# RWKV7 attention and a SoLU expert layer on one core: the head's first product in 64x64 tiles, an order of three tile shapes, and inverse steps in halves

## The chip, the cores and the metric

The kernel runs on one core of a Trainium2 chip. Five engines of that core work side by side, each on its own list of instructions: TensorE (PE, matrix products, with a separate row PEld for the loading of its weights), VectorE (DVE), ScalarE (ACT), GpSimd (POOL) and SyncE (SP), which here only issues DMAs. The metric is the time of one execution in microseconds (us), as the device measures it; lower is better.

## The reference

Two blocks follow one another. The first is a linear recurrence over 768 time steps, for 4 batches and 8 heads of 40 channels, all in fp32:

```
for t in range(S):
    y[:, :, t] = einsum('bhd,bhde->bhe', rt, state)
    Sa = einsum('bhde,bhe->bhd', state, at)
    state = state * wt[:, :, None, :] - einsum('bhd,bhe->bhde', Sa, bt) + einsum('bhd,bhe->bhde', vt, kt)
```

Its result, rearranged to 3072 tokens of 320 numbers (8 heads of 40), is `x` of the second block:

```
h = x @ w_in                                   # 3072 x 1024
e = exp(h - max(h)); solu = h * e / (sum(e) + 1e-9)
ln = (solu - mean(solu)) / sqrt(var(solu) + 1e-6) * g_ln
out = ln @ w_out                               # 3072 x 320
```

`w_in` (320x1024), `w_out` and `g_ln` arrive as float64 and are narrowed on the chip.

## The kernel before, in words

**Runs.** The sequence is cut into chunks of 64 tokens. A run is one chunk of two batches, so there are 24 runs (12 chunks, 2 pairs of batches) of 128 tokens each, and each is 16 units (2 batches x 8 heads) of 64 tokens by 40 channels. Within a run the recurrence is solved in closed form: the products of a and b of a unit's tokens make a triangular 64x64 matrix, whose inverse gives all of the run's updates at once; only the state goes from a run to the next one of its pair.

**Products of units.** A unit's matrices are at most 64x64, so `mm` (L276) issues them in 64x64 quarters of the 128x128 array, in an order that goes round the four quarters. Names of the groups on TensorE, which the profile uses: pu (solve), ps (scores), psr and px (the state's part), py (norm, which gives the triangular matrix nt, and couple), pz (close), pyo (read, in two parts: with lv and with lu). Transposes (L363) turn a, b, r, k, v, the decay ei and the state: pa, pb, pr, pkv, pst. pcum (L344) sums the logarithms of the decay.

**The inverse.** nt's two 32x32 diagonal blocks per unit are inverted on VectorE, for two runs at a time (GRP = 2): 64 blocks, in 12 inverses. The norm of a run is evicted as nt (L436) and written to DRAM by four DMAs (L444, on POOL but for runs 2 and 3, on SP). Once both runs are there, `blk` is read back with one block to a partition (L453). Then come 30 steps, a generator from which the schedule draws so many at a time. Step j multiplies one column of the block by the columns found (L469, into `prod`) and subtracts (L471):

```
m, n_c = Q - 1 - j, (j + 1) // 2
nc.vector.tensor_tensor(out=t, in0=nb[..j..], in1=u[:, 0:n_c, j:j + 1]..., op=ALU.mult)
nc.vector.tensor_tensor(out=u[:, 0:n_c, j + 1:Q], in0=u[...], in1=t, op=ALU.subtract)
```

A step works on n_c x m elements a partition, from 30 to 126. The result goes to DRAM by SP (L477), and `bring` (L490, L492) fetches each run's part of it back as tu and uh, also by SP, which waits for the write. `flip` (L498) transposes 32x32 blocks of tu.

**The head.** `leave` sums what a run read (tot, L656, VectorE), multiplies it by the decay into x (L664, two on POOL) and into the next state (L674, two on POOL), and moves x into xT, the tokens' channels on partitions (L669, L670: four DMAs on SP; `left`, L684 and L686: six on POOL, a slot later). `hidden` is h = x w_in, 128 tokens by 1024: two products with all 128 rows and one with 64 rows, for each 512 columns. Each fp32 product is two records on TensorE, so h has 12 records a run. Then follow nmax (L706, VectorE), exp (L714, ScalarE), the weighing of h by e (L722, VectorE), the Square that gives the spread (L735, ScalarE, written over h), var and rs (L736, L737), eight transposes of both halves (plnT, L747) with one eviction lnT (L750), the product po with w2 (L761, eight products, in two calls of four), its scaling by rs into osb (L765, ScalarE) and the output's DMAs (L768, SP).

**Order.** The order on every engine is written out by hand. A loop over slots i = -1 to 27 issues in slot i: solve and read of run i, the scores, couple, close and driven of run i+1, the front (a, b, decay, norm) of run i+5, h of run i-3 and the output of run i-4, besides loads of later runs. `bring(i+1)` and the loads of v and r (L299) stand at a slot's start, then w, b, a, k. A table `plans` says how many inverse steps VectorE does at each of six places of a slot (in steady slots 3 + 11, and 2 more in even ones, plus what is left of an inverse), and in the first slots where w_in and w_out are narrowed. The norm of an odd run begins the next inverse.

**PSUM.** There are four pairs of banks, A, B, C and h. A group that takes a pair waits until its last user is read. h and Square have pair h; pu, pa, py, pyo, pz and plnT share A; ps, po, pkv and pcum share B; px, psr, pst and pr share C.

Of the kernel before, what the change touches and what calls it, by code (L numbers as in the profile page):

```python
# [20 lines left out]
IN_ROWS = (((0, 80), (240, 280), (160, 168)), ((80, 160), (280, 320), (200, 208)), ((168, 200), (208, 240)))  # L21
# [3 lines left out]
LAG = 1  # L25
# [5 lines left out]
def shape_constants():  # L31
# [8 lines left out]
        neg_hi=-(row >= Q).astype(np.float64),  # L40
# [10 lines left out]
def kernel(  # L51
# [26 lines left out]
    NK = 3  # L78
# [5 lines left out]
    small = ctx.enter_context(tc.tile_pool(name="small", bufs=3))  # L84
# [33 lines left out]
    a_t = zeroed(nc.vector, "a", [P, H, C], 4, pad)  # L118
# [15 lines left out]
    nc.gpsimd.memset(above, 0.0)  # L134
    for x in range(Q // 2):
        nc.gpsimd.memset(above[:, x, 2 * x + 1:], -1.0)
    w_in = const.tile([P, 2 * NK - 1, DFF // 2], FP32, name="w_in")
# [15 lines left out]
    lands = [(0, 0), (1, 0), (2, 0), (0, 1), (1, 1)]  # L153
    landed = {}

    def land(n, queue):
# [3 lines left out]
        if n < len(lands):  # L160
            kt, x = lands[n]
# [5 lines left out]
            y = 0  # L167
            for at in (x,) if kt < 2 else (0, 1):
                for first, last in IN_ROWS[kt]:
                    queue.dma_start(out=to[y:y + last - first], in_=moe_w_in[first:last, 512 * at:512 * at + 512])  # L170
                    y += last - first
            landed[n] = [(w_in[:, 2 * kt + x], to, None)]
# [50 lines left out]
    def vector(plan, kept=0):  # L223

        for word in plan.split():
            if word in "bsf":
                dict(b=begin_narrow, s=scale_narrow, f=end_narrow)[word]()
            else:
                some(int(word), kept)

    def turn_g():
        pg = pair("B", "pg")[:, 0]
# [9 lines left out]
    def mean_of(lo, hi, begun, tag):  # L242
        t = pair(tag, "pmean")[:, 0]
        nc.tensor.matmul(t[:, 0:DM], lhsT=ident, rhs=begun, start=True, stop=False)
        mean_part(t, lo, hi, False)
        return mean_kept(t)
# [59 lines left out]
    def load_keys(i, names, queue=nc.sync):  # L306
        if not ok(i):
            return
        for n, ap in (("w", w), ("b", b), ("a", a), ("k", k)):
            if n in names:  # L310
                x = a_t[i % 4] if n == "a" else two.tile([P, H, D], FP32, tag="raw_" + n, name="raw_" + n,
                                                             bufs=3)
# [3 lines left out]
    def load_values(i):  # L316
# [4 lines left out]
        d["raw_r"] = two.tile([P, H, D], FP32, tag="raw_r", name="raw_r")  # L321
        load(d["lv"][:, :, C:], v, i)
        load(d["raw_r"], r, i, nc.gpsimd)
# [13 lines left out]
    def decay(i):  # L337
        if not ok(i):
            return
# [3 lines left out]
        t = (pair("B", "pcum")[:, 0] if i > 9 else h_pair("pcum"))[:, 0:DM]  # L343
        nc.tensor.matmul(t, lhsT=c_("cum"), rhs=d["lw"], start=True, stop=True)  # L344
        nc.scalar.activation(out=ei_t[0][:, :, 0:D], in_=heads(t), func=AF.Exp)
        inv = d["inv"] = two.tile([P, DM], FP32, tag="inv", name="inv", bufs=4)
        nc.scalar.activation(out=inv, in_=t, func=AF.Exp, scale=-1.0)  # L347
# [44 lines left out]
    def front_b(i, t=None, y=0):  # L392
# [5 lines left out]
        def evict():  # L398
            d["bT"] = kept("bT", t)
# [18 lines left out]
    def shared_pair(i):  # L418

        if i not in shared:  # L420
            shared[i] = pair("A", "py")
        return shared[i]

    def norm(i, first=lambda: None):
        if not ok(i):
            first()
# [8 lines left out]
        first()  # L435
        nc.scalar.copy(out=nt, in_=t[:, :, 4 * Q:4 * Q + 256].rearrange("p b (j c) -> p b j c", j=4))  # L436
# [3 lines left out]
        queue = nc.sync if 1 < i < 4 else nc.gpsimd  # L440
        for x in range(2):
            for e in range(2):
                home = C * x + Q * e
                queue.dma_start(out=blocks[n][e].rearrange("(a x h) s c -> a x s h c", a=GRP, x=2)[at, x],  # L444
# [11 lines left out]
    def invert(n):  # L456
# [8 lines left out]
        for j in range(1, Q - 1):  # L465
            m, n_c = Q - 1 - j, (j + 1) // 2
            prod = two.tile([P, Q * Q // 8], FP32, tag="prod", name="prod", bufs=1)
            t = prod[:, 0:n_c * m].rearrange("p (c r) -> p c r", c=n_c)
            nc.vector.tensor_tensor(out=t, in0=nb[:, j:j + 1, j + 1:Q].to_broadcast([P, n_c, m]),  # L469
# [498 lines left out]
```

## Time and profile before

| | |
|---|---|
| median of 3 executions | 579.21 us (579.07 to 583.95) |
| profiled execution, span | 580.2 us |
| busy in that span | PE 510.6, PEld 360.5, DVE 407.9, ACT 316.9, POOL 299.8 us |
| slot 0 begins (its pu) | 63.7 us |
| slots 0 to 4 | 115.7 us |
| slots 5 to 18 | 274.3 us, 19.6 each |
| slots 19 to 22 | 75.5 us |
| from 529.2 to the end | 51.0 us |

One execution was recorded by the hardware profiler, and all durations are from it; its span is a microsecond more than the median. A line such as "317.78 0.88 PE pu L276 x32" of the chain (what released what, followed back from the last instruction) says: from 317.78 us on, for 0.88 us, the end waited for PE's 32 records of the group pu, issued in line 276. In the rows of the timeline the tile's name is output<-inputs, followed by the shapes (partitions x elements), and the brackets name the idle time ahead and what ended it. PEclk is TensorE's granted clock as a share of its full speed. SPq, POOLq and the like are the issuing of DMAs on that engine's list.

### The profile page before, as it was taken

Reading aid. Unit: us, or ns where it says so; the run is one execution under the profiler, and the core shown is the slowest. Engines: PE = TensorE matmul, PEld = TensorE weight load, DVE = VectorE, ACT = ScalarE, POOL = GpSimd, SP = SyncE. Lnnn points to the kernel's source line nnn. Section 1 sums busy time; section 2 is a strip of 40 time slices with the busy share of each in tenths; the row PEclk is TensorE's granted clock in tenths of the full one; section 3 lists DMA queues with packets and bytes.
Section 4 is the critical chain, followed back from the end, with each engine's and each line's share of the span. In section 5 each row is a group of like instructions: output and inputs, shape, how many; then the busy total and the mean of one; then the engine's idle time right before and its main releaser. Section 6 shows DMA issues by size and latency. Waiting matters only on the chain.

```text
span 580.2 us, 25261 instructions
## 1 busy us (share of the span) xinstructions
PE 510.6 (88%) x10773; PEld 360.5 (62%) x10773; DVE 407.9 (70%) x1072; ACT 316.9 (55%) x618; POOL 299.8 (52%) x534
## 2 busy tenths in 40 slices
PE   4462764876989999999999999999999989999995
PEld 3241653654766777677667767777777657666543
DVE  4698986996894886877959869779688487332121
ACT  4633573755646565756566566656564455444533
POOL 4554484555635736648576467475773554233200
PEclk9656787879779999999999999999999989999999
DMA  7896886746605536637555475365431431311110
GB/s 152 151 155 135 175 183 114 148 94 113 112 16 124 111 74 134 118 63 141 103 104 114 90 143 113 65 137 105 99 77 39 106 74 32 62 33 27 27 24 23
DMA packets 188200, 56.71 MB, mean 98 GB/s; under 512 B 171680, under 2 KB 181512, under 8 KB 188088
## 3 DMA queue, kind: packets, MB, share of 16 engines
q1 hardware_dynamic: 173288, 36.98, 34.6%
q0 software_dynamic: 12368, 17.19, 12.9%
q8 instruction: 85, 1.39, 1.0%
q10 hardware_dynamic: 2432, 0.92, 0.8%
q14 instruction: 27, 0.22, 0.1%
HBM read 40.10 MB, written 10.22 MB: 87 GB/s over the span
## 4 chain that ended last, share of the span: by engine, by line
PE 65%; DVE 17%; DMA 9%; issue 3%; ACT 3%; SPq 2%; POOL 1%; ACTq 0%; DVEq 0%; POOLq 0%
PE h L276 19%; PE po L761 15%; PE px L276 5%; DVE uu L471 5%; DVE prod L469 5%; PE pyo L276 4%; DMA uu_dram<-uu 3%; PE py L276 3%; PE ps L276 3%; PE pu L276 3%; PE pz L276 2%; PE pkv L363 2%; DMA tu<-uu_dram 2%; PE plnT L747 2%; PE psr L276 2%
## 5 line engine op out<-in xcount | busy, mean ns | idle before, releaser
L276 PE MATMUL h<-w_in,xT 128*128 128x512 f32 (+1 forms) x288 | 123.6, 632 | 0.3
L761 PE MATMUL po<-w,lnT 128*128 128x320 f32 x384 | 118.2, 454 | 1.8 <-ACT lnT L750 1.8
L471 DVE TENSOR_TENSOR uu<-uu,prod 128x30 f32<-128x30 f32 (+4 forms) x360 | 106.2, 295 | 12.4
L469 DVE TENSOR_TENSOR prod<-blk,uu 128x30 f32<-128x30 f32 (+4 forms) x360 | 105.5, 293 | 11.4 <-POOL kb L356 0.7
L664 POOL TENSOR_TENSOR x<-tot,ex 104x256 f32<-104x256 f32 x48 | 32.3, 690 | 130.3 <-DVE tot L656 119.5
L761 PEld LDWEIGHTS po<-w,lnT 128*128 128x128 f32 x384 | 71.3, 194 | 31.9 <-issue 3.2
L444 POOL DMA_DIRECT2D nt_dram<-nt x88 | 52.3, 602 | 24.3 <-ACT c L734 21.4
L276 PEld LDWEIGHTS h<-w_in,xT 128*128 128x128 f32 (+1 forms) x288 | 40.4, 190 | 34.3 <-issue 29.1
L706 DVE TENSOR_REDUCE nmax<-h 128x1 f32<-128x1024 f32 x24 | 29.4, 1224 | 38.0 <-PE h L276 37.5
L510 ACT ACTIVATE wy<-py,cst 128x256 f32<-128x256 f32 x24 | 11.4, 474 | 79.0 <-PE py L276 79.0
L403 DVE TENSOR_TENSOR lu<-pu,cst 128x512 f32<-128x512 f32 x24 | 16.5, 688 | 51.6 <-PE pu L276 51.6
L686 POOL DMA_DIRECT2D xT<-x x96 | 48.7, 511 | 1.2 <-DMA blk<-nt_dram 1.2
L276 PE MATMUL py<-tu,nt 64*64 64x32 f32 x768 | 16.5, 226 | 28.0 <-DVE tot L656 11.6
L714 ACT ACTIVATE e<-h,nmax 128x1024 f32<-128x1024 f32 x24 | 26.8, 1117 | 20.4 <-DVE nmax L706 20.3
L299 POOL DMA_DIRECT2D raw_r<-in_r_dram x48 | 33.8, 707 | 1.4 <-issue 1.3
L276 PEld LDWEIGHTS py<-tu,nt 64*64 64x64 f32 x768 | 15.6, 145 | 30.3 <-issue 19.8
L344 PE MATMUL pcum<-lw,cst 128*128 128x320 f32 x48 | 21.7, 538 | 14.4 <-ACT lw L335 14.4
L737 POOL TENSOR_TENSOR rs<-var,mhalf 128x1 f32<-128x1 f32 x24 | 13.6, 567 | 39.5 <-ACT var L736 38.8
L356 POOL TENSOR_TENSOR kb<-raw_b,inv 128x320 f32<-128x320 f32 x24 | 21.1, 880 | 21.1 <-ACT inv L347 6.9
L722 DVE SCALAR_TENSOR_TENSOR e<-h,e 128x1024 f32<-128x1024 f32 x24 | 29.2, 1215 | 3.8 <-ACT e L714 3.8
L276 PEld LDWEIGHTS pu<-x,tu 64*64 64x64 f32 x768 | 19.5, 142 | 16.8 <-ACT kvT L536 13.7
L735 ACT ACTIVATE h<-e,mu 128x1024 f32<-128x1024 f32 x24 | 26.8, 1116 | 4.1 <-DVE e L722 4.1
(131 smaller groups left out, 1068.9 us busy)
## 6 DMA issues: line engine op xcount, KB each, us to landing
blk<-nt_dram POOLq DMA_DIRECT2D x22, 256.0 KB, 3.7
raw_w<-in_w_dram SPq DMA_DIRECT2D x48, 80.0 KB
a<-in_a_dram SPq DMA_DIRECT2D x48, 80.0 KB
raw_r<-in_r_dram POOLq DMA_DIRECT2D x48, 80.0 KB, 3.5
lv<-in_v_dram SPq DMA_DIRECT2D x48, 80.0 KB
out_dram<-osb SPq DMA_DIRECT2D x47, 80.0 KB
raw_b<-in_b_dram SPq DMA_DIRECT2D x44, 80.0 KB
raw_k<-in_k_dram SPq DMA_DIRECT2D x42, 80.0 KB
```

The lines of the kernel that those rows point to most:

```text
L276: nc.tensor.matmul(o, lhsT=lhsT, rhs=rhs, start=start, stop=stop, skip_group_check=True)
L299: queue.dma_start(out=x[half(p), :, 0:D], in_=ap[2 * bp + p, :, ci * C:(ci + 1) * C, :].rearrange("h t d -> t h d"))
L444: queue.dma_start(out=blocks[n][e].rearrange("(a x h) s c -> a x s h c", a=GRP, x=2)[at, x], in_=nt[home:home + Q].rearrange("p h j c -> p ...
L469: nc.vector.tensor_tensor(out=t, in0=nb[:, j:j + 1, j + 1:Q].to_broadcast([P, n_c, m]), in1=u[:, 0:n_c, j:j + 1].to_broadcast([P, n_c, m]) ...
L471: nc.vector.tensor_tensor(out=u[:, 0:n_c, j + 1:Q], in0=u[:, 0:n_c, j + 1:Q], in1=t, op=ALU.subtract)
L664: nc.gpsimd.tensor_tensor(out=x[0:W2, 2 * q:2 * q + 2].rearrange("p g (b t) -> p b g t", b=2), in0=by_q(tot, q)[:, :, :, 0:C], in1=ex[:, : ...
L686: nc.gpsimd.dma_start(out=xT[to:to + Q, 2], in_=x[at + P - 3 * D:at + D, 2])
L706: nc.vector.tensor_reduce(out=nmax, in_=d["h"], axis=AX.X, op=ALU.max, negate=True)
L714: nc.scalar.activation(out=e, in_=d["h"], func=AF.Exp, bias=d["nmax"], accum_out=d["esum"])
L722: nc.vector.scalar_tensor_tensor(out=d["e"], in0=d["h"], scalar=1.0 / DFF, in1=d["e"], op0=ALU.mult, op1=ALU.mult, accum_out=d["mu"])
L735: nc.scalar.activation(out=d["h"], in_=d["e"], func=AF.Square, scale=-float(DFF), bias=d["mu"], accum_out=sq)
L761: nc.tensor.matmul(t, lhsT=d["lnT"][:, f, :], rhs=w2[:, f, :], start=f == 0, stop=f == NF - 1)
```

## The change

1. **h in 64x64 tiles.** `w_in` is laid out as five groups of 64 rows, both halves of its columns on the two partition halves. `hidden(i, n)` issues for n = 0 to 4 four products of 64 rows by 64 tokens with 512 columns, one in each quarter of the array: 20 products of a run instead of 6. xT holds each group of channels twice, on both partition halves; `moved` writes it with six DMAs on SP, and `left` with six on POOL. The five parts of h are dealt out between the groups of units.
2. **The slot's order.** First all transposes (64 rows by 104 or 128 columns), then everything in 64x64 (h0, pu, ps, h1, psr, norm, h2, carried px, pyo with lv, h3, couple, h4, close, driven px, pyo with lu), then the two groups on the full array (pcum, po undivided).
3. **Inverse steps.** nt is negated when it is evicted, so steps add. Steps with fewer than three columns take one fused instruction for each column; the others are cut into two halves of the columns, two products and two sums.
4. **Engines.** x and the next state (four instructions) go from POOL to VectorE, osb and (from run 10 on) bT from ScalarE to VectorE. Of the four nt writes two go by SP and two by POOL (from run 4 on).
5. **PSUM.** plnT and Square take pair h, each in its turn; pu, py and pcum go to C, px and po to B, psr to A; pz shares py's pair.
6. **Places.** `bring(i+2)` stands at the end of slot i, after all that is left of its inverse's steps; the loads of v and r of run i+3, one run further ahead. The plans are dealt anew: 14 steps in odd and 16 in even steady slots. What stood before the loop for the scores of run 0 is done in slot -1, and w_in and w_out are narrowed at other places. Fewer buffers: raw_w 2 instead of 3, a 3 instead of 4, small ones 2 instead of 3. LAG counts anew (`c = i - LAG`): h is still that of run i-3.

The core of the diff:

```diff
     def norm(i):
-        nc.scalar.copy(out=nt, in_=t[...])
+        nc.scalar.mul(out=nt, in_=t[...], mul=-1.0)
-        queue = nc.sync if 1 < i < 4 else nc.gpsimd
         for x in range(2):
             for e in range(2):
+                queue = (nc.sync, nc.gpsimd)[e] if i > 3 else nc.sync if 1 < i else nc.gpsimd
...
     def invert(n):
         for j in range(1, Q - 1):
             m, n_c = Q - 1 - j, (j + 1) // 2
-            nc.vector.tensor_tensor(out=t, in0=nb[...], in1=u[:, 0:n_c, j:j + 1]..., op=ALU.mult)
-            nc.vector.tensor_tensor(out=u[:, 0:n_c, j + 1:Q], in0=u[...], in1=t, op=ALU.subtract)
+            if n_c < 3:
+                for c in range(n_c):
+                    nc.vector.scalar_tensor_tensor(out=u[:, c, j + 1:Q], in0=nb[:, j, j + 1:Q], scalar=u[:, c, j:j + 1],
+                                                   in1=u[:, c, j + 1:Q], op0=ALU.mult, op1=ALU.add)
+            else:
+                parts_ = ((0, n_c // 2), (n_c // 2, n_c))
+                for lo, hi in parts_:
+                    prod = two.tile([P, 72], FP32, tag="prod", name="prod")
+                    ...
+                    nc.vector.tensor_tensor(out=ts[-1], in0=nb[...], in1=u[:, lo:hi, j:j + 1]..., op=ALU.mult)
+                for x, (lo, hi) in zip(ts, parts_):
+                    nc.vector.tensor_tensor(out=u[:, lo:hi, j + 1:Q], in0=u[:, lo:hi, j + 1:Q], in1=x, op=ALU.add)
...
+    def leave(i, tot):
+        for q in range(2 * (ci < NCH - 1)):
+            nc.vector.tensor_tensor(out=by_q(state_of(i)[:, 1], q)..., op=ALU.mult)
         for q in range(2):
-            nc.gpsimd.tensor_tensor(out=x[...], ..., op=ALU.mult)
+            nc.vector.tensor_tensor(out=x[...], ..., op=ALU.mult)
+        moved(i, 0, nc.sync)
+
+    def moved(i, y, queue):
+        x, xT = st[i]["x"], st[i]["xT"]
+        at = C * y
+        queue.dma_start(out=xT[at:at + D, 0:4], in_=x[0:D])
+        queue.dma_start(out=xT[at + D:at + C, 0:4], in_=x[C:C + C - D])
+        for j in range(4):
+            queue.dma_start(out=xT[at + 16 * j:at + 16 * j + 16, 4], in_=x[C + C - D:C + D, j])
...
+    def hidden(i, n):
+        if n == 0:
+            d["h"] = pair("h", "h").rearrange("p a b -> p (a b)")
+        for y in range(2):
+            for x in (y, 1 - y):
+                mm(d["h"][half(y), 512 * x:512 * x + 512], d["xT"][half(x), n, half(y)], w_in[half(x), n],
+                   start=n == 0, stop=n == NK - 1)
...
-        nc.scalar.activation(out=d["h"], in_=d["e"], func=AF.Square, ...)
+        nc.scalar.activation(out=pair("h", "sq")..., in_=d["e"], func=AF.Square, ...)
-        t = pair("A", "plnT")
+        t = pair("h", "plnT")
-        nc.scalar.activation(out=osb, in_=t, func=AF.Copy, scale=d["rs"])
+        nc.vector.tensor_scalar(out=osb, in0=t, scalar1=d["rs"], scalar2=None, op0=ALU.mult)
```

The main loop after, without its first slots' special cases:

```
load_keys(j + 3, "w"); load_r(i + 3)
front, attend_r, folded, decay_turned, front_b, attend_kv    # transposes, and their evictions
vector(plan[0]); stated(i + 1); left(i - 1)
hidden(c, 0); solved(i); vector(plan[1])
load_keys(j + 2, "bak")
scores(i + 1); flip(i + 1)
hidden(c, 1); scaled(j + 1); stated_r(i + 1); norm(j)         # odd j: begins the next inverse
hidden(c, 2); carried(i + 1); read(i, 0)
load_values(i + 3); logged(j + 2); vector(plan[2])
hidden(c, 3); couple(i + 1); hidden(c, 4); highest(c)
close(i + 1); driven(i + 1); read(i, 1)
exped(c); vector(plan[3]); summed(i); vector(plan[4])
decay(j + 2); weighed(c); spreadof(c); by_value(i + 2)
some(Q, (i + 2) // GRP); bring(i + 2)                         # the rest of that inverse, then its way back
leave(i); vector(plan[5]); output(c - 1)
```

with the steady plans

```diff
-plan = plans.get(i, ("", "", "3", "", "11", "") if i % GRP else ("", "2", "3", "", "11", ""))
+plan = plans.get(i, ("4", "", "7", "1", "", "2") if i % GRP else ("4", "", "o10", "", "", "1"))
```

## Prediction

> **What bounds the kernel now.** I read the page's busy shares and chain shares first, then busy time by stage.
>
> ```profile
> PE 510.6 (88%) x10773; PEld 360.5 (62%) x10773; DVE 407.9 (70%) x1072; ACT 316.9 (55%) x618; POOL 299.8 (52%) x534
> PE 65%; DVE 17%; DMA 9%; issue 3%; ACT 3%; SPq 2%; POOL 1%; ACTq 0%; DVEq 0%; POOLq 0%
> ```
>
> TensorE leads, but VectorE and the DMA hold a quarter of the chain. The windows below are cut at the starts of slots 0, 5 and 19 (their pu) and at 529.2, where the last heads are left; columns: window, its length, busy us of PE, PEld, DVE, ACT and POOL (instructions), PEclk, DMA share, GB/s.
>
> ```profile
> 63.70:179.40 115.70, 87.47 (x2077) 66.66 (x2075) 94.29 (x247) 64.65 (x131) 67.29 (x111) 0.83 0.59 120
> 179.40:453.70 274.30, 273.70 (x6349) 195.63 (x6348) 216.35 (x574) 167.27 (x330) 165.41 (x290) 1.00 0.52 102
> 453.70:529.20 75.50, 72.72 (x1565) 50.16 (x1564) 39.06 (x98) 37.34 (x69) 30.01 (x55) 0.98 0.27 60
> 529.20:580.20 51.00, 44.84 (x285) 25.44 (x284) 11.52 (x15) 18.59 (x34) 6.59 (x12) 1.00 0.09 21
> ```
>
> In slots 5 to 18 PE is never idle (273.7 of 274.3): 14 slots of 19.6 us, with 15.5 of VectorE. There only PE's time counts. Slots 0 to 4 are bound elsewhere (VectorE 94 of 116, half clocks), and the end is a serial chain. The chain of one steady slot (317.8 to 337.4) is PE alone; part of it:
>
> ```profile
> 318.65 0.93 PE ps L276 x64
> 319.59 1.06 PE h L276 x4
> 320.64 0.45 PE pst L363 x16
> 321.09 0.45 PE pa L363 x16
> 321.54 1.91 PE h L276 x4
> ```
>
> **PE, part by part.** I compared each group's time with the spacing of its own records inside it. A full h pair streams in 4 x 0.427 = 1.71 and takes 1.91; the half-row pair 0.85 and takes 1.06; eight po records 2.15 and take 2.35; pu 0.72 and takes 0.88; psr 0.45 and takes 0.63. Where the tile's shape is the same as before it (ps after pu, pa after pst) nothing is lost. So about 0.17 us goes at each change of shape. The chain of a slot has ten changes: 19.6 = 17.7 streaming + 1.9. The new order has three (64x128, 64x64, full): 17.7 + 3 x 0.17 = 18.2, and with 0.1 for what is not counted **T = 18.3**, a gain of 1.3 per slot if PE stays the bound.
>
> h itself should cost the same: 20 matmuls of 64x64, two records each, four abreast, are 10 rounds of 0.427 = 4.3; before 8 full records + 2 rounds of half-row pairs = 10 x 0.427. That four run abreast is seen in pu (32 records of 104 columns in 0.72, four per 0.0895 us = 0.86 ns a column, the rate of po's 0.2685 for 320). No row has 64x64 groups at 512 columns: bounds 4.3 and, two abreast, 8.6. I take 4.3, by pu, the row of the same shape.
>
> **VectorE.**
>
> ```profile
> 300.04 0.69 DVE L403 TENSOR_TENSOR psi<-ps,cst 128x512 f32<-128x512 f32 x1 [0.24 <-PE ps L276]
> 300.65 0.68 DVE L403 TENSOR_TENSOR lv<-ps,cst 128x512 f32<-128x512 f32 x1
> ...
> 306.68 0.19 DVE L469 TENSOR_TENSOR prod<-blk,uu 128x30 f32<-128x30 f32 x1
> 306.90 0.19 DVE L471 TENSOR_TENSOR uu<-uu,prod 128x30 f32<-128x30 f32 x1
> ...
> 313.25 0.27 DVE L469 TENSOR_TENSOR prod<-blk,uu 128x110 f32<-128x110 f32 x1
> 313.56 0.27 DVE L471 TENSOR_TENSOR uu<-uu,prod 128x110 f32<-128x110 f32 x1
> ```
>
> 30 elements take 0.19, 110 take 0.27: 0.16 + 0.001 per element. A dependent one follows 0.035 after the end; psi and lv, independent, overlap by 0.08. A step has a mean of 87 elements, so before: 2 x (0.16 + 0.09 + 0.035) = 0.57, 17.0 an inverse. After, four instructions of 0.205: starts at 0, 0.12, 0.24, 0.36, and the next step at 0.48, since each half waits only for its own half. 26 x 0.48, four short ones of 0.23 to 0.35 and the start: 14.1. That saves 2.9 per inverse, 1.45 a slot. Moved to VectorE: x 2 x 0.34 (256 elements by the same formula, less the overlap), st 2 x 0.24, osb 0.45, bT 0.6 (as aT's 0.69, one input less): +2.2. Gone with them is the stretching of steps that ran against x and st on POOL (a 126-element step at 316.3 took 1.11 and 0.84 instead of 0.28): 11.6 us in 12 inverses, 0.5 a slot. VectorE goes from 15.5 to some 16, 16.6 with flip's waits: under T, hidden beside PE. ACT loses osb and bT and gains nothing.
>
> A rule speaks against the halves. The Trainium skill, "VectorE: DVE Perf Modes", section "The DRAIN you can't avoid", says that the next operation does not start until the pipeline is empty, and asks for fewer operations instead of fewer semaphores. By it a step of four instructions is 0.82 instead of 0.48. The trace disagrees in part: lv starts 0.08 before psi's end.
>
> **SP's queue** decides, I think, how much of PE's gain is kept.
>
> ```profile
> 295.95 1.91 SPq L477 DMA_DIRECT2D uu_dram<-uu  x2
> ...
> 302.73 0.99 SPq L490 DMA_DIRECT2D tu<-uu_dram  x2
> 303.76 0.91 SPq L492 DMA_DIRECT2D uh<-uu_dram  x2
> ```
>
> The inverse goes out in 1.9 (1.3 elsewhere), lands 4.9 later, and comes back as tu and uh; SP waits in between. In the new order this bring stands behind the forced end of the inverse and ahead of everything of the next slot: xT (now 6 on SP instead of 4, before the outputs), the loads of w, b, a, k, v, and two of the four nt writes (4 were POOL's). SP per two slots: ten load pairs 1.35 = 13.5, outputs 2.4, tu and uh 3.8, uu 1.6, nt 4 x 0.45 = 1.8, xT 12 x 0.65 = 7.8, the wait 4.9: 35.8 of 36.6. From the inverse's end in an even slot (16.2) through that list to the second run's nt write is 34.5; with 2.1 of landing and 4.2 for blk's issue and landing (0.54, 3.7), blk is there at 57.0. The next inverse's first operation stands on VectorE at 17.3 of the next even slot, ahead of osb, aT and bT: 36.6 + 17.3 = 53.9. So it is 3.1 late per pair. The stall shifts slot and queue alike and gives the next round more room: bounds 0 and 3.1 a pair; I take the middle, 1.55. **T = 19.1**, 0.5 gained per slot, with bounds 18.3 and 19.85 (where 2T holds the whole round).
>
> POOL loses x, st and two nt writes and gains two xT: its 11.8 busy a slot falls, and what it hides (kb, blk) stays hidden. raw_w and a with one buffer fewer cost nothing while SP is behind, since it loads later anyway; if not, they are in the 3.1.
>
> **The other stages.** Before slot 0: attend_kv(0), attend_r(0) and scores(0) move into slot -1, beside VectorE's and the first inverse's waits: -2, bounds 0 and -4. Slots 0 to 4: 80 inverse steps at 0.1 to 0.15 less are -8 to -12, the moved operations 5 x 1.3 = +6.5, fewer half clocks: -4, bounds -12 and +4, for VectorE is 82% busy there. Slots 19 to 22 have no more loads, and took 22.5, 17.9, 17.9 and 17.1 (the first with 2.8 idle and 3.4 at half clock): after, 4 x 16.8 = 67.3 instead of 75.5, -8, since no inverse is late there; bound -3. The tail's period, from one h to the next, is h 4.97, nmax 1.24, exp 1.22, weighing 1.25, Square 1.25 = 10.06. Now the transposes and their eviction use h's PSUM pair ahead of the next h: +0.65 + 1.05, while h, all 64x64, needs 0.6 less: 11.1, times nearly four: +4, bounds +1 and +6.
>
> **Sum**, on the profiled 580.2: -2 - 4 - 14 x 0.5 - 8 + 4 = 563. The median of three is 1.0 below the profiled span: **562**.
>
> **Rivals.**
> *PE holds throughout* (0.20): blk is early because SP's issues are shorter than their means; T = 18.4: 14 x 0.7 more gives 552, and slots 0 to 4 with 2 more 550. For it: DMA share 0.52, so the queue is not bandwidth. Against: the 35.8 of 36.6.
> *The round takes it all* (0.13): T = 19.85, and slots 0 to 4 bound by the same round, no gain: -2 + 3.5 - 8 + 4 = 577.5, so 577.
> *Slower: the clock* (0.18). SP's load pairs have steady means of 1.32 to 1.61; with them the list is 37.1 instead of 35.8, and late blk stops VectorE, then PE through aT and bT. From an idle time of some 1.8 us on, the clock halves:
>
> ```profile
> 168.16 1.08 PE L276 MATMUL py<-tu,nt 64*64 64x32 f32 x32 [1.84 <-DVE tot L656]
> 170.07 4.63 PE L761 MATMUL po<-w,lnT 128*128 128x320 f32 x8
> ```
>
> Here 1.84 idle is followed by 6.8 us at half clock (po 4.63 instead of 2.35), 3.3 lost. Once a pair, at the even slot's end, with the stall of 1.55: T = 18.3 + (1.55 + 3.3) / 2 = 20.7, 14 x 1.1 = +15, slots 0 to 4 at -2: -2 - 2 + 15 - 8 + 4 = +7, **587**. It decides between 1.55 and 1.84, which is close; an idle time of 0.5 at 269.6 cost no clock.
> The Trainium skill, "TensorE: Matmul & The Clock Gate", section "Why this matters for your kernels", allows idle gaps up to about 3 us; by it this case would lose only the stall and end near 563. The trace disagrees: 1.84 was enough.
> *Halves that don't overlap* (0.04): each instruction waits out the one before as the dependent pair at 306.7 does, and a step is 4 x 0.24 = 0.96 instead of 0.57, +0.39 x 26 / 2 = 5 a slot on VectorE, 21.6 with its waits: T = 22, 14 x 2.4 = +34, and +12 in the head: about 625.
> *h not four abreast* (0.03): +4.3 a slot where PE is the bound, T near 22.6: some 630.
>
> **Chances.** The forecast 0.42 (552 to 572), the rivals as given. A per cent, 5.8 us, is about what a measurement here tells from no change. Faster by over 1%: the forecast and PE holding, 0.62; within 1% (574 to 585): the round's 0.13 and the clock's lower end, 0.02, together 0.15; slower: the rest of the clock's 0.16, and the last two, 0.23. The range, 546 to 588, takes in the first four cases and leaves out 2 in 10: the last two, the clock's upper half, and PE with the head's bound of -12.
>
> **What would show it.** Right: pu to pu 19.1 in the steady slots; ten rounds of h at 4.3 to 4.4; three jumps of 0.17 a slot; steps at 0.47; at the ends of even slots an idle PE of 1 to 2 us behind VectorE's wait for blk, and SP without a pause but that for uu. T of 18.4 and no wait on blk would mean the queue was overrated; half clocks in the steady slots, the slower rival; a tail under 54, that the shared pair costs nothing. Wrong altogether if VectorE is busy over 18 us a slot, or the first five slots take over 120.

## The result, and the profile after

The changed kernel takes **606.56 us** (median; 600.84 to 608.89 in 4 executions), the kernel before 580.35 beside it. The ratio is **1.0436, 95% interval 1.0373 to 1.0500**: 4.4% slower, where 562 was forecast. The profiled execution has a span of 607.1 us against 580.2. Cut at the same points as before (the first record of pu in slots 0, 5, 19 and 23):

| stage | before | after | difference | forecast |
|---|---|---|---|---|
| before slot 0 | 63.7 | 66.8 | +3.1 | -2 |
| slots 0 to 4 | 115.7 | 112.9 | -2.8 | -4 |
| slots 5 to 18 | 274.2 | 299.1 | **+24.8** | -7 |
| slots 19 to 22 | 75.5 | 71.3 | -4.2 | -8 |
| from slot 23 to the end | 51.1 | 57.0 | +5.9 | +4 |

Nearly the whole error lies in the 14 steady slots. The page of the changed kernel (busy times; TensorE's clock in 40 slices; the shares of the chain that ended last):

```profile
PE 499.0 (82%) x11445; PEld 365.3 (60%) x11445; DVE 447.4 (74%) x1801; ACT 301.3 (50%) x581; POOL 224.8 (37%) x402
PEclk9999865989999999979999989979999999999998
PE 49%; DVE 18%; DMA 13%; ACT 11%; SPq 5%; issue 3%; POOL 1%; ACTq 0%; DVEq 0%; POOLq 0%
```

TensorE is busy 11.6 us less than before, but its share of the chain fell from 65% to 49%: DMA, ScalarE and SP's issuing took its place. The same windows as before, with busy times of PE, PEld, DVE, ACT and POOL, then PEclk, DMA share and GB/s:

```profile
66.78:179.68 112.90, 79.91 (x2143) 63.32 (x2147) 97.47 (x385) 63.20 (x125) 47.85 (x83) 0.85 0.64 125
179.68:478.74 299.06, 270.10 (x6717) 198.35 (x6717) 243.28 (x1014) 155.45 (x302) 117.28 (x200) 0.97 0.50 100
478.74:550.07 71.33, 67.34 (x1668) 49.76 (x1664) 42.48 (x154) 34.89 (x64) 18.87 (x37) 1.00 0.25 59
550.07:607.10 57.03, 46.77 (x396) 29.17 (x388) 14.94 (x22) 16.61 (x29) 6.19 (x12) 0.97 0.10 25
```

Now PE has 29 us without work in the steady stage, where it had 0.6. What it waited for there (engine, line, tile; releaser; us in total, times, longest):

```profile
PE pkv L371 <- DVE osb L782: 18.4, 5, 5.6
PE py L277 <- ACT lu L649: 7.2, 7, 1.4
```

The first row is five even slots of the seven. Three of them also halve the clock. One such slot, from 327.3 to 354.5, shows how. First SP's issues of that round (start, duration; "x" is how many DMAs):

```profile
301.91 1.31 SPq L496 DMA_DIRECT2D uu_dram<-uu  x2
306.46 1.77 SPq L509 DMA_DIRECT2D tu<-uu_dram  x2
...
332.19 2.08 SPq L785 DMA_DIRECT2D out_dram<-osb  x2
334.38 1.40 SPq L300 DMA_DIRECT2D raw_w<-in_w_dram  x2
335.88 2.45 SPq L300 DMA_DIRECT2D raw_b<-in_b_dram  x2
338.37 1.31 SPq L300 DMA_DIRECT2D a<-in_a_dram  x2
339.78 2.02 SPq L300 DMA_DIRECT2D raw_k<-in_k_dram  x2
341.90 1.08 SPq L454 DMA_DIRECT2D nt_dram<-nt  x2
343.07 1.28 SPq L300 DMA_DIRECT2D lv<-in_v_dram  x2
344.45 1.32 SPq L496 DMA_DIRECT2D uu_dram<-uu  x2
```

Then POOL's side of the same nt (in brackets the idle time before, and what ended it):

```profile
333.48 1.22 POOL L454 DMA_DIRECT2D nt_dram<-nt  x2 [3.11 <-ACT nt L446]
344.79 1.08 POOL L463 DMA_DIRECT2D blk<-nt_dram  x2 [9.34 <-DMA nt_dram<-nt]
```

VectorE's rows where blk is wanted:

```profile
348.38 0.68 DVE L473 TENSOR_TENSOR uu<-blk,above 64x512 f32<-64x512 f32 x1 [5.08 <-DMA blk<-nt_dram]
350.55 0.25 DVE L479 SCALAR_TENSOR_TENSOR uu<-blk,uu 128x30 f32<-128x30 f32 x1 [1.34 <-DMA blk<-nt_dram]
350.72 0.54 DVE L782 TENSOR_SCALAR osb<-po,rs 128x320 f32<-128x320 f32 x1
351.18 0.68 DVE L398 TENSOR_TENSOR aT<-pb,ex 104x512 f32<-104x512 f32 x1
```

and PE's, which wait for them:

```profile
351.32 0.67 PE L371 MATMUL pkv<-cst,kb 64*104 64x64 f32 x8 [5.55 <-DVE osb L782]
352.77 1.98 PE L277 MATMUL h<-w_in,xT 64*64 64x512 f32 x8
```

POOL writes its half of nt at 333.48, at once after the eviction; SP's half goes out at 341.90, because SP is still busy with its list. Both are needed, so blk is issued at 344.79 and is there at 350.5. VectorE could have begun at 343.3. Behind the inverse's first operations stand osb, aT and bT, and pkv needs the pair B that osb empties. PE idles 5.55 us, and the next h runs at half clock (1.98 for two rounds instead of 1.04).

From one uu (301.91) to the next (344.45) SP's round takes **42.5 us**, and apart from the 3.2 it waits for uu it never pauses for more than 0.4. The five rounds from 213.76 to 435.17 take 43.1, 45.0, 42.5, 44.8 and 45.9 us, while two undisturbed slots of this kernel (18.8 each) would need 37.6. The stall goes with how late SP's half of nt is: in the four even slots where it goes out 4.8 to 8.4 us behind POOL's half, PE then stands for 2.4 to 5.6 us; in the two where it goes out less than 2 us behind, for 0.5 us at most.

### The profile page after: what moved, and what is told of

Its sections match the earlier page's. It is cut to its first block, busy times and chain, and to the rows that moved or that the text cites. A ratio compares the mean times of both kernels' runs of the same rounds, so it can differ in the third digit from the quotient of the medians.

```text
span 607.1 us, 27381 instructions
## 1 busy us (share of the span) xinstructions
PE 499.0 (82%) x11445; PEld 365.3 (60%) x11445; DVE 447.4 (74%) x1801; ACT 301.3 (50%) x581; POOL 224.8 (37%) x402
## 3 DMA queue, kind: packets, MB, share of 16 engines
q1 hardware_dynamic: 184560, 39.28, 35.8%
## 4 chain that ended last, share of the span: by engine, by line
PE 49%; DVE 18%; DMA 13%; ACT 11%; SPq 5%; issue 3%; POOL 1%; ACTq 0%; DVEq 0%; POOLq 0%
PE h L277 15%; PE po L780 10%; DMA blk<-nt_dram 6%; PE py L277 5%; PE px L277 5%; DVE prod L487 4%; DVE uu L490 3%; PE pyo L277 3%; SPq L300 3%; PE ps L277 2%; DMA nt_dram<-nt 2%; ACT sq L756 2%; PE pu L277 2%; PE pcum L349 2%; ACT lnT L771 1%
## 5 line engine op out<-in xcount | busy, mean ns | idle before, releaser
L277 PE MATMUL h<-w_in,xT 64*64 64x512 f32 x960 | 131.4, 609 | 6.2 <-ACT lnT L771 6.2
L487 DVE TENSOR_TENSOR prod<-blk,uu 128x60 f32<-128x60 f32 (+21 forms) x624 | 112.8, 221 | 2.3
L490 DVE TENSOR_TENSOR uu<-uu,prod 128x60 f32<-128x60 f32 (+21 forms) x624 | 113.7, 222 | 0.0
L780 PEld LDWEIGHTS po<-w,lnT 128*128 128x128 f32 x384 | 73.1, 192 | 36.6 <-issue 4.2
L727 DVE TENSOR_REDUCE nmax<-h 128x1 f32<-128x1024 f32 x24 | 29.3, 1222 | 40.5 <-PE h L277 40.4
L454 POOL DMA_DIRECT2D nt_dram<-nt x48 | 29.6, 620 | 71.4 <-ACT nt L446 71.4
L277 PEld LDWEIGHTS h<-w_in,xT 64*64 64x64 f32 x960 | 34.8, 134 | 13.9 <-ACT lnT L771 7.3
L649 ACT COPY lu<-pu 128x320 f32<-128x320 f32 x24 | 10.2, 425 | 62.0 <-DVE lu L415 62.0
L277 PE MATMUL py<-aT,bT 40*64 40x64 f32 x768 | 19.5, 248 | 25.4 <-ACT lu L649 24.1
L349 PE MATMUL pcum<-lw,cst 128*128 128x320 f32 x48 | 24.4, 597 | 15.7 <-ACT lw L340 15.7
L463 POOL DMA_DIRECT2D blk<-nt_dram x22 | 11.8, 543 | 67.3 <-DMA nt_dram<-nt 65.3
L756 ACT ACTIVATE sq<-e,mu 128x1024 f32<-128x1024 f32 x24 | 26.8, 1118 | 16.3 <-DVE e L743 16.3
L277 PEld LDWEIGHTS py<-aT,bT 40*64 40x64 f32 x768 | 16.2, 158 | 30.6 <-ACT lu L649 25.6
```

The source lines that it names most:

```text
L277: nc.tensor.matmul(o, lhsT=lhsT, rhs=rhs, start=start, stop=stop, skip_group_check=True)
L487: nc.vector.tensor_tensor(out=ts[-1], in0=nb[:, j:j + 1, j + 1:Q].to_broadcast([P, hi - lo, m]), in1=u[:, lo:hi, j:j + 1].to_broadcast([P, ...
L490: nc.vector.tensor_tensor(out=u[:, lo:hi, j + 1:Q], in0=u[:, lo:hi, j + 1:Q], in1=x, op=ALU.add)
L727: nc.vector.tensor_reduce(out=nmax, in_=d["h"], axis=AX.X, op=ALU.max, negate=True)
L756: nc.scalar.activation(out=pair("h", "sq").rearrange("p a b -> p (a b)"), in_=d["e"], func=AF.Square, scale=-float(DFF), bias=d["mu"], acc ...
L780: nc.tensor.matmul(t, lhsT=d["lnT"][:, f, :], rhs=w2[:, f, :], start=f == 0, stop=f == NF - 1)
```

## Experiments

All ratios are to the kernel before, run beside. "Steady" is the length of slots 5 to 18 in the profiled execution (274.2 before, 299.1 after).

**1. nt on POOL again.** The only edit to the changed kernel:

```diff
-                queue = (nc.sync, nc.gpsimd)[e] if i > 3 else nc.sync if 1 < i else nc.gpsimd
+                queue = nc.sync if 1 < i < 4 else nc.gpsimd
```

> The kernel after, with all four nt writes of a run on POOL again (from run 4 on), nothing else changed. Theory (place in SP's list): the two SP writes stand behind outputs and four pairs of loads and go out 8.4 us after the POOL ones (341.9 against 333.5), so blk is late; on POOL they go out at once, blk lands some 9 us after nt's eviction, before VectorE wants it. Then even slots lose their stall and their half clocks: 14 slots of 18.9 instead of 299.1 us, so 607.1 - 34 = about 573 (568 to 580). Rival A (SP's round of two slots is full whatever stands in it, the wait for uu in it): only 2.2 us a pair go, the stall of some 6 shrinks by a third: about 592 to 598. Rival B (blk's own landing of 5.1 us is the trouble): the stall stays at 2 us or more a pair, with half clocks: 590 to 600.

Measured: 582.27 us, ratio 0.9998 (0.9960 to 1.0035); steady 273.3. Two DMAs a run, moved from SP to POOL, bring back 24 of the 26 us. The five waits of pkv fall from 18.4 to 0.3 us and the clock is 1.00 throughout:

```profile
180.00:455.00 275.00, 266.70 (x6784) 195.67 (x6778) 241.01 (x1010) 155.31 (x302) 138.68 (x236) 1.00 0.57 111
```

But the 573 expected is missed: the slots stay at 19.5 instead of 18.9. With this edit alone the new order is as fast as the old one, not faster.

**2. The same writes ahead of SP's loads.** Place or length of the list?

```diff
-        load_keys(j + 2, "bak")
         scores(i + 1)()
...
         norm(j)
+        load_keys(j + 2, "bak")
```

> The kernel after, nt writes still two on SP and two on POOL, but the loads of b, a and k (three pairs on SP, 4 to 6 us) are issued behind them instead of ahead. Theory (place in SP's list): the SP writes go out some 5 us earlier, blk lands 5 to 6 us earlier, the stall of up to 7.9 us falls to 0 to 2: 575 to 588. Rival A (the round is full): the same instructions stand on SP, so the round is as long and the time stays within 1% of 607. Rival B (blk's landing): falls in between, no more than 10 us gained.

Measured: 605.16, ratio 1.0411 (1.0357 to 1.0465); steady 298.6. This place explains nothing. PE waits as before:

```profile
PE pkv L371 <- DVE osb L782: 17.6, 6, 6.0
```

Since SP still had the same list in a round, everything on it, and the next bring, came as late as before: its five rounds from 212.95 on take 42.2 to 44.3 us, without a pause of over 0.5 us but that for uu, and its half of nt, though three load pairs earlier in the list, still goes out 2.9 to 6.7 us behind POOL's.

**3. Less on SP's list, nothing on another.** The changed kernel with nt split as it was, and four of SP's six xT moves left out (the first 512 columns of h use channel group 3 twice in place of group 4, whose channels are left out there; PE does the same work):

```diff
-        for j in range(4):
+        for j in range(4 * y):
             queue.dma_start(out=xT[at + 16 * j:at + 16 * j + 16, 4], ...)
...
-                mm(..., d["xT"][half(x), n, half(y)], w_in[half(x), n], ...)
+                mm(..., d["xT"][half(x), n if x else min(n, 3), half(y)], w_in[half(x), n], ...)
```

> The kernel after, nt split as it was, with the same four moves left out (the first 512 columns of h use group 3 twice in place of group 4). Theory (SP's list: 43 us a pair with the wait for uu, of which 5.3 go): the stalls ahead of blk shrink to nothing or below 1 us, the half clocks go, steady slots 18.9 to 19.5: 574 to 584 instead of 606. Rival (the SP write's place behind the loads costs in itself): stalls of 2 to 5 us stay in even slots, 590 to 600.

Measured: 582.63, ratio 1.0030 (0.9989 to 1.0071); steady 275.1. nt still goes by SP, behind the loads, and the stall is gone: VectorE waits for blk 1.8 us in all instead of some 23, PE for osb 0.5. SP's half of nt now goes out at most 1.5 us behind POOL's in the even slots, for example:

```profile
323.00 1.23 POOL L454 DMA_DIRECT2D nt_dram<-nt  x2 [3.25 <-ACT nt L446]
324.01 1.08 SPq L454 DMA_DIRECT2D nt_dram<-nt  x2
```

This is the clearest of the runs: **the length of SP's list** is the cause, and 5.3 us a pair less is enough. It also moves less data, but run 1 moves all of it and loses the stall too, so less traffic is not what does it.

**4. The same with nt on POOL.**

> The kernel after with nt writes on POOL, and four of SP's six xT moves of a run left out (2.6 us of issuing a slot): the last 64 channels of x are not moved to the first partition half, so the first 512 columns of h use the channels of group 3 twice in place of those of group 4. All instructions of other engines are unchanged. Theory (SP's list alone holds 19.5): the steady slots come down to 18.8 to 19.0, 14 slots 264 to 267 instead of 273.3, 572 to 577 in all. Rival (VectorE's list stands right there too): 19.3 or more, 579 to 584.

Measured: 579.92, ratio 0.9967 (0.9925 to 1.0009); steady 272.9. SP's idle times over 0.3 us now add up to 85 us in 275 (41 in run 1), and the slots don't follow. So after run 1 SP's list was full but no longer the bound: the theory falls for what is left above 18.8, and the rival's number came, though its reason is tested in the next two.

**5. Is it VectorE's list?** Run 1 with x and the next state back on POOL, and run 1 with whole inverse steps (one product, one sum):

```diff
-            nc.vector.tensor_tensor(out=by_q(state_of(i)[:, 1], q)..., op=ALU.mult)
+            nc.gpsimd.tensor_tensor(out=by_q(state_of(i)[:, 1], q)..., op=ALU.mult)
-            nc.vector.tensor_tensor(out=x[0:W2, 2 * q:2 * q + 2]..., op=ALU.mult)
+            nc.gpsimd.tensor_tensor(out=x[0:W2, 2 * q:2 * q + 2]..., op=ALU.mult)
```

> The kernel after with all nt writes on POOL (as in the run before) and, besides, x and the next state (four instructions) back on POOL: VectorE has 1.9 us a slot less to do. Rival (VectorE's order is what now holds the steady slots at 19.5, since PE needs 18.8): they fall to about 18.9, the total by 8 to 10, to about 572. Theory (SP's list is full: in the steady slots it pauses only for the inverse's landing, so a pair of slots takes what SP takes): VectorE's relief moves nothing, or x comes later from POOL and the time grows: 580 to 590.

> The kernel after with nt writes on POOL, and the inverse steps whole again (one product, one sum; negated nt kept). This prices the halves in the new order. Theory (VectorE's list stands right below SP's at 19.5): whole steps take 2.9 us an inverse more, 1.45 a slot, the steady slots rise to some 20.5 to 21, and slots 0 to 4 by up to 8: 595 to 605. Rival (only SP's list binds): the steady slots stay at 19.5, and 582 to 590 in all.

Measured: 583.84, ratio 1.0034 (0.9991 to 1.0078), steady 271.6; and 583.74, ratio 1.0044 (1.0016 to 1.0072), steady 273.3. VectorE's busy time in the window 180 to 455 is 221.6 in the one, 241.5 in the other and 241.0 in run 1, and the slots are the same within 0.12 us. Busy time leaves out the short pauses between dependent instructions; with them (those under 0.08 us) the steps take 133.6 us of that window when whole and 119.6 in halves. So whole steps did lengthen VectorE's list, by 1.0 us a slot, and the slots did not follow. VectorE's list is not the bound of run 1 either; the halves are worth nothing in these slots.

What is left is PE itself. In run 1 it is busy 266.7 of 275 us, and what it waits for is small and many-sided, at most 1.7 us at a time; the three largest, between 150 and 480 us:

```profile
PE py L277 <- ACT lu L649: 5.7, 6, 1.4
PE pb L371 <- ACT r L335: 2.0, 3, 1.7
PE po L780 <- ACT x L634: 1.1, 4, 0.3
```

The first is new: norm's py and pu now share pair C, and py starts when lu has been evicted, half by VectorE and half by ScalarE. What undoing it would give was not tested.

**6. SP's moves on other queues.** Six xT moves from SP to POOL; with nt on POOL as well; and that with x and state on POOL and the tail of run 8:

```diff
-        moved(i, 0, nc.sync)
+        moved(i, 0, nc.gpsimd)
```

> The kernel after with only the six xT moves of a run taken from SP to POOL's queue; the nt writes stay split between SP and POOL. Theory (SP's list is full, and the nt writes are late because everything on it is): SP loses 4.5 us a slot, 9 a pair, so it pauses again; nt goes out in time from SP too, the stalls before blk go, the steady slots fall to PE's 18.8 to 19.1 and the total to about 570 to 576. Rival (VectorE's order holds them): 19.4 and more, as with nt on POOL: 580 or more. Rival (a write by SP is late by its place alone): part of the stall stays, 585 to 600.

> Both: nt writes and xT moves on POOL's queue. By the theory (SP's list) SP has room to spare in either case, so this is within 1% of the kernel with xT alone moved, 568 to 576; if POOL's queue, with some 16 DMAs a slot, fills up in its turn, blk's issue is late again and the time lies above it, 575 to 590.

> As the first of these four, but with SP's six xT moves on POOL's queue instead of ScalarE's: POOL then issues nt, both xT sixes, blk and r and computes x, state, kb and rs, some 19 us a slot. Theory: POOL's list is then the full one, 19.5 or more a slot, and its DMA issuing stretches VectorE's steps (129 us of steps in the steady slots with xT on POOL, 120 without): 575 to 588, above the other.

Measured: 590.27 (1.0121; 1.0039 to 1.0202, steady 278.1), 586.04 (1.0090; 1.0053 to 1.0128, steady 275.9), 591.20 (1.0164; 1.0120 to 1.0208, steady 290.7). The first two take back most of the stall. The third takes back a third of what the steady slots had lost and shows the fault again on the next list: POOL is busy 202 of 275 us, and VectorE waits 15.7 us for a late blk.

**7. SP's moves on ScalarE.** First directly behind x's computation (with nt, x and the state on POOL, and run 8's tail), then at a place where x has long been there:

```diff
-        moved(i, 0, nc.sync)
+        moved(i, 0, nc.scalar)
...
         norm(j)
+        if ok(i - 1):
+            moved(i - 1, 0, nc.scalar)
```

> Both bounds at once: nt writes on POOL, the six xT moves of SP issued by ScalarE instead, x and the next state on POOL (VectorE's list 1.9 us a slot shorter), and the tail with plnT on pair A and Square on pair C for runs 20 to 23. Theory (two lists stand one behind the other at some 19.5: SP's, and, once that is eased, VectorE's): only with both eased do the steady slots come down to PE's 18.8 to 19.0: 14 slots about 265 instead of 273, and 575 (nt, xT and tail without VectorE's relief: 578) falls to 562 to 570. Rival (a third list, ScalarE's with 4.5 us of issuing a slot more, or POOL's, holds them): 19.4 or more, 572 to 582.

> The kernel after with nt writes on POOL, and SP's six xT moves issued by ScalarE a slot later, behind nt's eviction, where ScalarE waits some 3 us for py anyway. POOL's and VectorE's lists are unchanged. Theory (SP's list alone holds 19.5): SP pauses again, the steady slots come down to 18.8 to 19.0, 14 slots about 266 instead of 273.3, 572 to 577 in all. Rival (VectorE's list holds them too): 19.4 and more, 580 to 584. Rival (ScalarE's issuing of 4.5 us delays wy and the couple): slots of 20 and more, 588 or above.

> As the first of these, with whole inverse steps. If VectorE's list is what binds once SP has room, the 2.9 us an inverse come back here: 1.0 to 1.45 a slot more than with halves, 586 to 597. If TensorE binds (VectorE's list fits into 18.9), less than 0.3 a slot more, within 5 us of the other.

> As the first of these, but nt split between SP and POOL as in the kernel after: only xT leaves SP's list. Theory (the split cost what it cost because SP's list was full): no stall before blk, within 1% of the first. Rival (an SP write is late by its place behind the loads): stalls of 2 us and more in even slots with half clocks, 585 or above.

> As the first of these, with x and the next state on POOL (VectorE's list 1.9 us a slot shorter) and the tail with plnT on pair A and Square on pair C. If VectorE's list is the next bound: steady slots at 18.8 to 19.0 here and not in the first, 560 to 570. If neither: the tail's 7 alone, 565 to 575.

Measured: the first 738.25 (ratio 1.2702; 1.2651 to 1.2754). There x, computed on POOL, stood behind rs, which needs Square; ScalarE stood waiting for x with rT behind it, 7 us a slot. That was a fault of my placing and says nothing of SP. The others: 626.53 (1.0775; 1.0676 to 1.0873), with whole steps 629.29 (1.0841; 1.0758 to 1.0924), with split nt 647.36 (1.1126; 1.1003 to 1.1249; VectorE waits 0.2 us for blk there, so with xT off SP's list split nt makes no stall ahead of blk, but the 21 us above the first of these are not explained), with all eased 616.90 (1.0605; 1.0490 to 1.0720). ScalarE's rows in the last of these:

```profile
300.60 0.60 ACT L446 ACTIVATE nt<-py 128x512 f32<-128x512 f32 x1
300.75 0.80 ACTq L699 DMA_DIRECT2D xT<-x  x1
301.59 0.79 ACTq L700 DMA_DIRECT2D xT<-x  x1
302.41 3.46 ACTq L702 DMA_DIRECT2D xT<-x  x4
305.93 0.47 ACT L340 ACTIVATE lw<-raw_w 128x320 f32<-128x320 f32 x1 [4.72 <-DMA xT<-x]
```

Six issues hold ScalarE for 5.1 us. The wy that the couple and all behind it needs comes that much later, and PE waits for it up to 4.0 us a slot (19.5 in 13 of them). The rival "ScalarE's issuing delays wy" was right. Neither POOL's list nor ScalarE's took SP's six moves without a loss (on POOL, with nt there too, the steady slots took 275.9 in run 6 against 273.3 in run 1).

**8. The tail.** Both xT and nt on POOL, and for runs 20 to 23:

```diff
-        t = pair("h", "plnT")
+        t = pair("A" if i >= N - 4 else "h", "plnT")
-        nc.scalar.activation(out=pair("h", "sq")..., func=AF.Square, ...)
+        nc.scalar.activation(out=pair("C" if i >= N - 4 else "h", "sq")..., func=AF.Square, ...)
```

> As the last one, and for runs 20 to 23 the transposes plnT take pair A and Square pair C, which nobody uses by then, instead of pair h. Theory of the tail (h's pair is held through Square, transposes and eviction: 1.25 + 0.73 + 1.02 more between one h and the next): the period falls from 11.5 us to about 9.8 (h 4.6, po 4.5, plnT 0.7, PE without idle times), four periods, and the half clock at the end goes with the idle time: 7 to 11 us less than the kernel it is built on. Rival (the chain nmax, exp, weighing, Square bounds the period by itself): 0 to 4 less.

Measured: 578.04, ratio 0.9942 (0.9912 to 0.9972). From slot 23 to the end 49.7 us instead of 57.1 in the kernel it is built on: 7.4, at the low end of what was expected. It is a version of the new order that beats the old one, by half a per cent.

**9. One part alone in the kernel before.** nt split between SP and POOL; and the new inverse steps (the code of the diff's `invert`, with negated nt):

> The kernel before with one part of the change alone: nt writes two on SP and two on POOL from run 4 on. Theory (place): in the order of before SP has issued its loads and xT by the time nt is evicted and only the output stands behind, and blk is wanted 7 us after its issue, so the split costs nothing: 577 to 583. Rival A (SP's round is the bound by itself): 2.2 us more a pair on a list that already waits for uu, late blk or late tu, 590 or more. Rival C (a write by SP is slow in itself, with all other traffic in its rings): blk's issue, 5.5 us behind nt's in before, comes 2 us or more later, with 0 to 15 us in the total.

> The kernel before with the inverse steps of after (negated nt, sums, fused short steps, two halves of columns), nothing else. Theory (halves overlap, PE bounds the steady slots): a step falls from 0.57 to 0.48 us, VectorE's busy time per inverse measured from first to last step falls from 17.0 to about 14.5, the steady slots stay at 19.6, slots 0 to 4 lose 80 x 0.1 = 8 us at most: 570 to 579. Rival (more instructions contend with POOL's: x, st and kb on POOL stretch more of them): steps in slots with POOL busy take longer than before and the total is 580 or more.

Measured: 584.89, ratio 1.0069 (1.0019 to 1.0120), steady 273.4; and 577.45, ratio **0.9914 (0.9882 to 0.9946)**, steady 274.3. Split nt makes no stall in the old order: its steady stage is as long as without (the 0.7% lies outside that stage or in the spread of the executions; the profiled one shows 580.1). There too SP's list was about full: three of its rounds (39.8, 38.7 and 40.5 us, against 39.2 for two slots) have no pause of over 0.5 us but that for uu. The halves gain 4.5 us in slots 0 to 4 (111.2 instead of 115.7) and nothing in the steady slots.

**10. A better kernel before.** The last one, and Square of runs 20 to 23 on pair C:

```diff
-        nc.scalar.activation(out=d["h"], in_=d["e"], func=AF.Square, ...)
+        nc.scalar.activation(out=pair("C", "sq")... if i >= N - 4 else d["h"], in_=d["e"], func=AF.Square, ...)
```

> The kernel before with the inverse steps of after, and Square of runs 20 to 23 written to pair C instead of over h, so that the next h waits for the weighing alone. Theory: the tail's period (10.06) loses Square's 1.25 but shows plnT's 0.65 ahead of the next h, so 0.6 to 1.2 for each of four: 2 to 5 less than with the steps alone (577.5): 572 to 576.

Measured: **573.63, ratio 0.9850 (0.9788 to 0.9913)**: the lowest of all, though its interval overlaps that of the halves alone (0.9882 to 0.9946), so that the edit's own worth is not shown. If it has one, it is not for the reason given: the tail took 52.3 us instead of 51.1 (its period fell from 10.06 to 9.84, and the last po ran at half clock, 6.28 instead of 4.59). What went in the profiled execution is the stall in slot 19 (2.8 us in the kernel before, 2.2 with the halves alone) and the half clock behind it, to which the edit does nothing that I can name. That part is not explained.

## Why the prediction was wrong, point by point

**SP's queue.** The right place and the right chain (late nt by SP, late blk, VectorE's first inverse operation ahead of osb and aT, PE idle at the end of even slots), with its size wrong. The step that failed is the term "SP per two slots ... 35.8 of 36.6". It had 30.9 of issuing and 4.9 of waiting. The round from 301.91 to 344.45 has 36.9 of issuing, 3.2 of waiting and 2.4 of gaps of 0.1 between issues, which the sum did not have at all: 42.5. Nearly every row was longer than its best case: outputs 1.9 and 2.1 instead of 1.2 a pair of DMAs, xT 4.1 to 5.0 for six instead of 3.9, load pairs 1.27 to 2.45 where 1.35 was set. I had the slower means (1.32 to 1.61) and gave them to a rival instead of to the forecast. And the upper bound, 3.1 of lateness a pair, was worked out from the same sum, so it was no bound: VectorE waited up to 6.4 us in one slot. A second term of the lateness was short as well: blk's issue and landing took 5.7 (344.79 to 350.5) instead of 4.2.

**The middle of two bounds.** "The stall gives the next round more room, so half of it" was argued, not read. The trace bears it out in part: behind the stall of 4.65 the next round has 5.7 us of pauses beside that for uu, and the next stall is 0.45; but the stall of 5.55 is followed by one of 5.34. Run 3 shows the steepness: 5.3 us less on the list takes 24 us out of 14 slots, because a stall behind a full list costs the idle time and the half clock after it.

**The rival that came.** "Slower: the clock" (0.18, 587) named the mechanism that happened. Its price was short: T = 20.7 against 21.4 measured, 14 x 1.1 = 15 against 24.8. Its parts here: 18.4 us of idle PE, and three half clocks of about 6.8 us each, which cover 15.0 us of PE's busy time and so cost 7.5. With 14 x 18.8 = 263.2 of clean slots and 10.5 of PE's smaller waits these make 299.6, where the stage took 299.1.

**PE's gain.** The mechanism holds and the size is off. The chain of an undisturbed slot of the changed kernel, from 221.9 on:

```profile
221.93 0.71 PE pu L277 x32
222.64 1.12 PE ps L277 x64
223.76 0.86 PE h L277 x8
224.63 0.47 PE psr L277 x32
225.09 0.47 PE py L277 x32
225.56 0.86 PE h L277 x8
...
232.22 0.74 PE pcum L349 x2
232.96 4.30 PE po L780 x16
```

h takes 0.86 for two rounds, just the streaming time: four 64x64 groups do run abreast at 512 columns, and the rival of 630 is out. pu is 0.71 instead of 0.88, psr 0.47 instead of 0.63, po 4.30 instead of 4.70. But the slot is 18.8, not 18.3: pcum still pays 0.2 as the first full group, ps takes 1.12 where it took 0.93 before, and the transposes take 2.4 with a pause in them. The gain is 0.8 instead of 1.3 a slot, and in run 1 0.7 of it goes again, most of it to the small waits shown there (PE is idle for 8.3 of 275 us).

**Halves.** The step time is right:

```profile
326.49 0.34 DVE L487 TENSOR_TENSOR prod<-blk,uu 128x60 f32<-128x60 f32 x2
326.75 0.34 DVE L490 TENSOR_TENSOR uu<-uu,prod 128x60 f32<-128x60 f32 x2
327.01 0.35 DVE L487 TENSOR_TENSOR prod<-blk,uu 128x56 f32<-128x56 f32 x2
```

A row here is a pair of halves; pairs follow every 0.26, a step takes 0.52, and my formula gives 0.54 for its 60 elements. The rule of the Trainium skill ("VectorE: DVE Perf Modes", "The DRAIN you can't avoid") would have four instructions of 0.22 one after the other, 0.88; these rows don't agree with it. VectorE's other terms were a little low: x 0.76 for the two instead of 0.68, osb 0.55 for 0.45 and bT 0.68 for 0.60. The stretched steps were misread: the one at 316.3 in the kernel before (1.11) ran while POOL computed kb (316.38 to 318.13), which the change leaves on POOL. Steps beside x and the next state are no longer stretched, those beside kb still are (a pair at 328.86 took 1.59 us instead of 0.34). All in all VectorE is busy 17.4 us a steady slot instead of some 16, and hidden even so. The forecast counted on the halves in slots 0 to 4, for 8 to 12 us of steps; run 9 gives 4.5 there and nothing in the steady slots, and by run 5 the steady slots do not need them even with VectorE's new work.

**The head and the tail.** Up to slot 5 the forecast was -6, measured +0.3: of the 2 us that were to go ahead of the loop nothing shows, pu of slot 0 starts 3.1 later. Which step failed there stays open. The tail was +5.9 for +4: the period is 11.54 instead of 11.1, and the last po ran at half clock (6.28). Its step, the shared pair h, is shown by run 8. Slots 19 to 22 gained 4.2 of 8: they took 17.8 instead of the 16.8 that PE's gain was to give. One sum of a rival is off too, without a bearing on the rest: the terms given for 625 make 620 (580.2 - 2 + 12 + 34 - 8 + 4).

## What to carry to other kernels

Where several DMA queues are fed by hand, add up each issuing engine's list for a whole period, with mean rows, gaps between issues and the waits inside it, before moving a DMA onto it; when the sum comes within some per cent of the period, treat the change as slower, because anything late is late for everyone behind it. If a list is too full, shuffling its order does not help (run 2). Shorten it (here 5 us a pair of slots were worth 24 us in 14 slots), or move work to a list that has room, by the same sum: POOL's took two DMAs a run at no loss (run 1), but SP's six xT moves besides cost something there (run 6) and much on ScalarE's (run 7). A bound worked out from the same optimistic sum as the forecast is no bound.

## What the runs showed of the hardware

- An issue of a DMA held the issuing engine, on all three engines used for it: 0.5 to 0.56 us for xT on POOL, 0.8 to 0.87 on ScalarE, 0.73 as a mean on SP. On SP, over all DMAs of the changed kernel's steady slots, half took 0.6 us or less and one in ten 1.1 or more, up to 1.86, and consecutive issues left 0.05 to 0.1 between them.
- TensorE's clock did not follow the length of one idle time by the threshold that I had taken from 1.84 us: 2.41 us idle (217.5 to 219.9) left it at 1.00, and 4.65, 5.55 and 5.34 halved it, from 2.4 to 4.2 us into the idle time, for 6.8 us each. The Trainium skill ("TensorE: Matmul & The Clock Gate", "Why this matters for your kernels") puts the limit near 3 us of idle time; these four agree with it, the 1.84 us of the kernel before do not, nor do 2.78 us there (464.2 to 467.0, half clock from 468.4 on). Within an execution all changes of the clock lie a whole number of steps of 3.41 us apart; in the steady slots of the changed kernel they are at 262.88, 269.70, 348.21, 355.04, 396.00 and 402.82. So where an idle time falls between these points may count beside its length: of 2.41 us no more than 1.37 lay in one step, of 1.84 and 2.78 it was 1.73 and 1.96. This does not settle it: an idle time of 2.17 (175.64 to 177.81), with 1.91 in one step, cost no clock.
